# Another order for a planned attention-and-gate kernel: 117 instead of 133 changes of the array mode, the first pairs' bounds in two parts, the last output tile in two halves

## The chip, the cores and the metric

The kernel runs on one core of a Trainium2 chip. The metric is the device time of one execution in microseconds (us), as a median over executions. Of one further execution there is a profile by the hardware profiler, with the start and duration of each instruction and the landing of each transfer.

A core has five engines with a queue each: TensorE (PE in the profile; its weight loads are PEld), VectorE (DVE), ScalarE (ACT), GpSimd (POOL) and SyncE (SP), which here issues nearly all DMA transfers. An engine executes its queue in order and waits on semaphores of the others. So the order in which a program hands instructions to each engine is part of the program, and this case is about that order.

## The reference

For 4 batches, 8 heads, 768 positions and 64 features, keys are cut into 24 chunks of 32. For every query, an upper bound of its scores in each chunk is worked out from the chunk's smallest and largest key in each feature. The six chunks with the largest bounds (among the chunks that are not in the future) are kept, and softmax attention runs over them under the causal mask. The heads, side by side, are the input x of a gated unit:

```python
ub = np.sum(np.maximum(q * k_min, q * k_max), axis=-1)        # [.., 768, 24]
ub = np.where(causal, ub, -1e9)
top_chunks = np.argsort(ub, axis=-1)[..., -6:]
scores = where(chosen chunk & causal, scale * q @ k.T, -1e9)
x = softmax(scores) @ v                                       # [4, 768, 512]
gate = sigmoid(sum over 5 taps of conv_w[k] * x shifted by 4 - k)
out = (gate * (x @ w_val)) @ w_out                            # [4, 768, 512], float32
```

## The kernel before

**Tiling.** Two heads make a pair, so there are 16 pairs, and four pairs make a batch. For pair p the program creates some 60 operations, each of which is a short run of instructions on one engine. The names below are used in all that follows; the number of the pair stands behind the name, and digits behind that count parts.

- kn, qn, vn: the pair's loads (SP, lines 457 and 460). ktr, qtr: transposes of K and Q on TensorE (line 472). kev, qev: their evictions by ACT (478, 514). kred: chunk maxima and minima on DVE (484). ksm: the small arithmetic on those by GpSimd (504 to 509).
- rhi, qlo, rlo: relu(Q) and the low-order parts of Q and relu(Q), on ACT or DVE (522 to 565). Bounds must be exact enough to order chunks, so each is a sum of four products: relu(Q) high, Q high, Q low, and relu(Q) low, with chunk values. Four matmul terms form ub (590, or 605 for the pairs 0 to 3, whose form lies in `ubd`). qsb is one matmul that helps ACT to get at Q's low part in pairs 1 to 3 (530).
- top, cmp: the sixth largest bound and the comparison with it, on DVE. selT (663) transposes the comparison on TensorE, and mc copies it to SBUF, on ACT or DVE (675, 677); from pair 9 on a transposing DMA, md, does both (665).
- sc p.0 to p.5: scores of the pair in six PSUM-bank groups (692), with the selection added as a large negative number by a second matmul (697). Each is 64 rows of contraction, two heads side by side, which is a row-tiled mode of the array. ex: the exponentials by ACT (706), twelve per pair. tri: the causal diagonal by GpSimd (714). av: P times V on TensorE (735). nrm: the division, on DVE (743, 744).
- tox and xc, or from pair 8 to 14 one transposing DMA xd (765): the result transposed to xT. xw writes xT to a scratch in DRAM (778), xs reads it back in another layout into XS (782), and cv, the convolution of the gate, is 40 matmuls on tiles of 64 rows by 32 columns (793): a third mode of the array. th: the sigmoid as a tanh, on ACT (799).
- Per batch: val (816), gv (824), out (840), oe, which evicts an output tile (847, 850), and od, its store (855).

**PSUM.** There are eight banks. A score group takes two, a convolution two, and most others one, until what reads them is done.

**What sets the order.** `graph` creates the operations with their dependencies, an estimated duration and a key. The key is the number of the pair times `PERIOD`, plus an offset of the stage from `OFF`, plus one of the stage and pair from `DELTA`. `Graph.schedule` is a list scheduler: in a modelled time it starts, on each engine that is free, the ready operation with the lowest key, if a PSUM bank is free. It adds `MODE_SWITCH` where TensorE goes from one array mode to another; `mode` is "row" for sc, "col" for cv and none for all others. Then `plan` hands on the order, `fill` puts idle-time matmuls on a zero tile into TensorE's early gaps (915), and the operations are emitted in that order, so all the numbers above affect the program through the order alone, and through how many fillers fit.

The beginning also holds eight matmuls on the zero tile (line 345). In the bounds of the pairs 0 to 3, the four terms of each of five query tiles stand together:

```python
terms = [(rh, 0), (Qh, 1), (ql, 1), (rl, 0)]      # for tile i: two matmuls each
```

and the first matmul of pair 0, with the causal fill, is `identb` times `cfill`. The last output tile (batch 3, tile 5) is like every other: four matmuls of 512 columns, one eviction by DVE, one store by SP.

Of the kernel before, what the change touches and what calls it, by code (L numbers as in the profile page):

```python
# [14 lines left out]
AF = mybir.ActivationFunctionType  # L15
# [39 lines left out]
for _bi, _segs in enumerate(BANKS):  # L55
    for _col, _jt, _q0, _n in _segs:
        for _i in range(_n // 128):
# [5 lines left out]
PERIOD = 13.2487  # L63
OFF = dict(wdg=689.463, wbig=-821.57, cw=-638.386, load=-26.611, ktr=-313.189, qtr=-239.905, kev=166.913,
           qev=-383.955, ksm=148.208, spl=244.528, vc=540.922, ub=-278.308, top=-291.823, selT=-172.354,
           sc=-256.234, ex=-198.66, av=-117.315, nrm=263.685, tox=-134.594, xs=14.333, conv=-269.157,
           tanh=-393.525, val=323.303, gv=522.471, out=327.173, ev=91.258)
# [3 lines left out]

EARLY = (0, 1, 2)
# [6 lines left out]
    wdg=(-0.259, 11.176, 5.417, 0.077, -1.668, 4.13, 5.35, 1.029, 15.805, 3.045, -3.731, 0, -3.953, 0, 0, 0),  # L79
    wbig=(4.521, -1.173, -4.251, -0.71, -6.836, -7.879, -1.406, -13.108, -0.554, -12.202, 1.098, -1.574,  # L80
        -2.473, -1.919, 10.286, 15.067),
    cw=(0, 0, 1.049, 0, -3.776, -0.311, -0.92, -4.993, -0.92, -6.529, -7.915, -11.168, 0.948, 0, -8.06, 3.706),
    load=(-9.433, -20.842, -32.131, -6.001, -15.044, -1.827, -12.02, 13.514, 5.014, 13.589, 14.754, 5.081,
        -6.414, 4.609, -2.48, -7.659),
    ktr=(-2.8, -5.035, -2.262, 2.581, 0.902, 9.564, 0, 0, 10.923, 1.13, -0.491, -0.903, 0, 13.091, 0, -1.519),
    qtr=(0, -0.071, 9.102, 0, 3.757, 12.574, 5.717, -4.881, -3.114, -14.91, -6.366, 2.222, 0.471, 9.573, 4.53,
        0),
    kev=(-2.229, -2.16, 2.677, -4.88, -7.568, -10.347, 4.307, -2.668, 4.622, 3.276, -0.858, 6.192, 2.689,
        -4.962, -5.387, -2.214),
    qev=(-4.798, -6.316, 0, 0.959, 0, -3.801, -4.226, -3.069, -0.528, -1.223, 0, 0, -6.763, 0, 2.363, 0.065),  # L90
    ksm=(13.028, 3.364, 1.499, 0.759, -1.548, -11.855, -3.051, 6.295, -16.352, 0.972, -0.612, 7.732, 0, -1.146,
        0, -2.064),
# [193 lines left out]

ENG = ("PE", "ACT", "DVE", "POOL", "SP")
SEM = dict(PE=0.20, ACT=0.17, DVE=0.15, POOL=0.11, SP=0.0)
MODE_SWITCH = 0.04
DMA_HEAD, DMA_TAIL, DMA_QUEUE = 1.0, 1.3, 3.0  # L290


# [4 lines left out]
def act(n):  # L297
    return 0.051 + n / 1200.0
# [732 lines left out]
```

## Time and profile before

| | us |
|---|---|
| median of 4 runs | 189.7 |
| their range | 188.59 to 191.15 |
| the profiled execution's own time | 190.39 |
| its span, first to last instruction | 188.7 |
| TensorE busy (2994 matmuls) | 177.7 |
| ACT busy | 145.1 |
| DVE busy | 137.6 |
| GpSimd busy | 88.1 |

The granted TensorE clock was 1.000 as a mean over the span. Of the page's parts, the share of busy time tells which engine is nearest to its limit as a mean, and the row of 40 slices where along the span that holds. The chain is followed back from the last instruction and says on what the end hung. The waits say what an engine with nothing to do was waiting for. A line of the timeline has a start, a duration, engine, line, operation, output and input, the count of equal instructions that were merged, and in brackets the idle time of that engine before it. Matmuls overlap in their pipeline, so the start of one to the start of the next is what one costs, and that is shorter than the duration shown.

### The profile page before, as it was taken

What the parts mean: (1) busy time and instruction counts of PE and PEld (TensorE: products, weight loads), DVE (VectorE), ACT (ScalarE), POOL (GpSimd) and SP (SyncE); (2) the same over time, 40 slices, a digit from 0 to 9 for tenths busy, and PEclk for the clock granted to TensorE, in tenths of its full rate; (3) what the DMA queues carried; (4) which work ended last, traced back from release to release, by engine and by line L of the source; (5) the groups of instructions that cost most, each with busy time, mean ns of one, the idle gap of its engine ahead of it and who ended that gap; (6) DMA issues with size and microseconds to landing.
All of it is one profiled execution on the core that took longest, in us unless ns stands there. A gap on an engine that the chain in (4) does not pass through costs nothing.

```text
span 188.7 us, 7611 instructions
## 1 busy us (share of the span) xinstructions
PE 177.7 (94%) x2994; PEld 118.1 (63%) x2994; DVE 137.6 (73%) x452; ACT 145.1 (77%) x326; POOL 88.1 (47%) x187
## 2 busy tenths in 40 slices
PE   7889999999999999999999999999999897799992
PEld 2566768777687658667766766767665654444540
DVE  4696998799989997999996889797965322521551
ACT  4659999989979788799939998969999596156221
POOL 5336899998981851715154563538464021000000
PEclk9999999999999999999999999999999999999999
DMA  6999999999699998988998999999959979977335
GB/s 141 220 218 218 215 208 181 221 199 211 185 216 261 235 224 198 212 216 242 140 231 210 233 201 223 104 226 148 227 136 218 244 237 199 271 252 250 116 121 212
DMA packets 97105, 38.77 MB, mean 206 GB/s; under 512 B 86810, under 2 KB 91950, under 8 KB 97070
## 3 DMA queue, kind: packets, MB, share of 16 engines
q1 hardware_dynamic: 95966, 37.25, 93.9%
q0 software_dynamic: 1104, 1.05, 3.9%
q8 instruction: 23, 0.38, 0.9%
q14 instruction: 12, 0.10, 0.2%
HBM read 27.34 MB, written 9.47 MB: 195 GB/s over the span
## 4 chain that ended last, share of the span: by engine, by line
PE 75%; ACT 7%; DMA 7%; DVE 6%; issue 2%; SPq 1%; ACTq 0%; DVEq 0%
PE b L735 11%; PE b L692 11%; PE b L816 10%; PE b L472 10%; PE b L840 9%; PE b L793 8%; PE b L697 7%; PE b L590 5%; DMA XS<-scr 5%; ACT P L706 4%; DMA qn<-in_q_dram 2%; PE b L663 1%; DVE km L484 1%; PE b L760 1%; ACT Qh L514 1%
## 5 line engine op out<-in xcount | busy, mean ns | idle before, releaser
L706 ACT ACTIVATE P<-b 128x512 f16<-128x512 f32 (+2 forms) x192 | 88.9, 597 | 6.2 <-PE b L697 2.2
L714 POOL TENSOR_SCALAR_AFFINE_SELECT P<-P 128x512 f16<-128x512 f16 (+1 forms) x64 | 34.0, 552 | 43.9 <-ACT P L706 43.8
L692 PE MATMUL b<-Qh,Kh 64*128 64x128 f16 (+3 forms) x384 | 39.9, 259 | 0.6 <-ACT P L706 0.6
L697 PE MATMUL b<-MT,E 64*128 64x128 f16 (+4 forms) x352 | 37.0, 255 | 0.1
L484 DVE TENSOR_REDUCE km<-b 128x12 f32<-128x384 f32 x64 | 32.4, 547 | 6.0 <-PE b L472 3.5
L824 DVE SCALAR_TENSOR_TENSOR gv<-g,b 128x384 f16<-128x384 f32 x32 | 17.1, 548 | 15.7 <-PE b L816 14.0
L735 PE MATMUL b<-VA,P 128*128 128x65 f16 x672 | 27.7, 194 | 0.0
L735 PEld LDWEIGHTS <-P 128*128 128x128 f16 x672 | 24.4, 98 | 4.3 <-issue 2.3
L692 PEld LDWEIGHTS <-Kh 64*128 64x128 f16 x384 | 17.7, 94 | 12.8 <-issue 8.0
L799 ACT ACTIVATE g<-b 128x384 f32<-128x384 f32 x32 | 14.1, 497 | 14.1 <-PE b L793 14.0
L816 PE MATMUL b<-xT,wval 128*128 128x384 f16 x128 | 24.5, 327 | 0.0
L840 PE MATMUL b<-wout,gv 128*128 128x512 f16 x96 | 23.0, 379 | 0.0
L850 ACT ACTIVATE osb<-b 128x512 f32<-128x512 f32 x21 | 12.9, 639 | 10.6 <-PE b L840 6.7
L697 PEld LDWEIGHTS <-E 64*128 64x128 f16 x352 | 17.3, 94 | 4.6 <-issue 1.9
L793 PE MATMUL b<-XS,WD 64*32 64x384 f16 x640 | 16.5, 324 | 2.9 <-DMA XS<-scr 1.9
L478 ACT ACTIVATE Kh<-b 128x384 f16<-128x384 f32 x32 | 16.0, 532 | 3.7 <-PE b L472 2.9
L744 DVE TENSOR_TENSOR on<-b,rcp 128x384 f16<-128x384 f32 x32 | 17.8, 557 | 1.1
L514 ACT ACTIVATE Qh<-b 128x384 f16<-128x384 f32 x32 | 15.2, 508 | 3.1 <-PE b L472 3.0
L816 PEld LDWEIGHTS <-wval 128*128 128x128 f16 x128 | 11.4, 98 | 9.9 <-issue 2.6
L560 DVE SCALAR_TENSOR_TENSOR rl<-Qh,ql 128x640 f16<-128x640 f16 x16 | 14.4, 901 | 2.2 <-ACT ql L537 2.2
L472 PE MATMUL b<-ident,qn 128*128 128x128 f32 x96 | 14.7, 281 | 0.3 <-DMA qn<-in_q_dram 0.3
L472 PE MATMUL b<-ident,kn 128*128 128x128 f32 x96 | 14.3, 281 | 0.7 <-DMA kn<-in_k_dram 0.5
(87 smaller groups left out, 287.3 us busy)
## 6 DMA issues: line engine op xcount, KB each, us to landing
XS<-scr SPq DMA_DIRECT2D x32, 194.0 KB, 4.2
kn<-in_k_dram SPq DMA_DIRECT2D x32, 192.0 KB, 4.8
qn<-in_q_dram SPq DMA_DIRECT2D x32, 192.0 KB, 4.4
vn<-in_v_dram SPq DMA_DIRECT2D x16, 384.0 KB, 5.3
out_dram<-osb SPq DMA_DIRECT2D x24, 256.0 KB, 3.6
scr<-xT SPq DMA_DIRECT2D x32, 97.0 KB, 4.3
wvn<-in_moe_w_val_dram POOLq DMA_DIRECT2D x1, 512.0 KB, 8.4
wout<-in_moe_w_out_dram POOLq DMA_DIRECT2D x4, 128.0 KB, 7.5
```

What stands on the lines that cost most here:

```text
L472: t.nc.tensor.matmul(out=b[:, j * 128:(j + 1) * 128], lhsT=vv(name, p)[:, 3 * w + j, :], rhs=t.ident, is_transpose=True, start=(j == 0), s ...
L484: t.nc.vector.tensor_reduce(out=vv("km", p)[:, i, w * 12:(w + 1) * 12], in_=bank(("kn", p, w))[:, 0:HB].rearrange("p (c t) -> p c t", t=CH ...
L692: nc.tensor.matmul(out=bb[hh][:, col:col + n], lhsT=kh[HP[hh], jt * 128:(jt + 1) * 128], rhs=qh[HP[hh], q0:q0 + n], start=(si == 0), stop= ...
L697: nc.tensor.matmul(out=bb[hh][:, col + m0 - q0:col + n], lhsT=t.E[HP[hh], jt * 128:(jt + 1) * 128], rhs=mt[HP[hh], m0 - 128:q0 + n - 128], ...
L706: t.nc.scalar.activation(out=t.P[p % 2][hh][bi], in_=bank(("s", p, bi, hh))[:, 0:n], func=AF.Exp, scale=0.125 / QS)
L714: t.nc.gpsimd.affine_select(out=ap, in_=ap, pattern=[[0, n], [1, 128]], compare_op=ALU.is_ge, fill=0.0, base=0, channel_multiplier=-1)
L735: t.nc.tensor.matmul(out=b[:, qt, :], lhsT=t.P[p % 2][hh][bi][:, col:col + 128], rhs=vv("VA", p)[:, hh, jt, :], start=(jt == 0), stop=(jt ...
L744: t.nc.vector.tensor_tensor(out=vv("on", p)[:, :, hh * 64:(hh + 1) * 64], in0=b[:, :, 0:D], in1=rc.unsqueeze(2).to_broadcast([128, NT, D]) ...
L793: t.nc.tensor.matmul(out=bank(("cv", p, r))[32 * g:32 * g + 32, 0:HB], lhsT=t.WD[HP[r], g * 20 + k * 4 + p % 4, :], rhs=x[HP[r], g * XH + ...
L816: t.nc.tensor.matmul(out=k[:, 0:HB], lhsT=t.wval[:, ct, et * 128:(et + 1) * 128], rhs=t.xT[:, (4 * b_ + ct) % 8, XL + w * HB:XL + (w + 1) ...
L824: t.nc.vector.scalar_tensor_tensor(out=vv("gv", 4 * b_ + et)[:, sl], in0=vv("g", 4 * b_ + et)[:, sl], scalar=1.0, in1=bank(("val", b_, et, ...
L840: t.nc.tensor.matmul(out=k, lhsT=vv("gv", 4 * b_ + et)[:, s * 128:(s + 1) * 128], rhs=t.wout[:, et, :], start=(et == 0), stop=(et == NCT - 1))
```

## The change

1. `MODE_SWITCH` goes from 0.04 to 0.09, some estimated durations change (cwrep 0.7 to 1.5, wsplit 1.3 to 1.7, wout 2.0 to 2.2, ktr and qtr 0.33 to 0.35), and `PERIOD`, all of `OFF` and all of `DELTA` are replaced. Every engine's order is another one.
2. For pair 0, the stages from ktr to selT have fixed keys ahead of everything else (`FIRST`).
3. For the pairs 0 to 3 the bounds are emitted as ub (three terms, all five tiles) and then ur (the fourth term, relu low, all five tiles), so ub need not wait for rlo.
4. The copy mc of pair 0 is made by DVE and no longer by ACT (`MCA`).
5. The last output tile is made in two column halves: four matmuls of 256 columns each, the first evicted by DVE and stored by SP, the second evicted by ACT and stored from ACT's queue. The output tiles 2 to 5 of the last batch have keys behind everything else.
6. Seven instead of eight matmuls on the zero tile at the beginning.

```diff
-PERIOD = 13.2487
-OFF = dict(wdg=689.463, wbig=-821.57, ...
+PERIOD = 14.0000
+OFF = dict(wdg=1118.545, wbig=-917.674, ...
+FIRST = dict(ktr=0, qtr=1, kev=1, ksm=2, qev=2.5, spl=3, ub=4, top=5, selT=6)
+MCA = (1, 2)
...
-MODE_SWITCH = 0.04
+MODE_SWITCH = 0.09
...
     def key(stage, p, x=0.0):
+        if p == 0 and stage in FIRST:
+            return FIRST[stage] - 100 + x
         return p * period + off[stage] + off.get((stage, p), 0.0) + x
...
-        for _ in range(8):
+        for _ in range(7):
             t.nc.tensor.matmul(out=b, lhsT=t.warm[:, 0:128], rhs=t.warm, start=True, stop=True)
...
-        def ubd(i, p=p):
+        def ubd(i, low, p=p):
...
-                if i == 0:
+                if i == 0 and not low:
...
                 for k, (lhsT, m) in enumerate(terms):
+                    if low != (k == 3):
+                        continue
...
             for i in range(NIT):
-                G.op(f"ub{p}.{i}", "PE", 0.28 + (0.14 if i == 0 else 0), key("ub", p, 0.02 * i), ubd(i),
...
+                o = G.op(f"ub{p}.{i}", "PE", 0.21 + (0.14 if i == 0 else 0), key("ub", p, 0.02 * i), ubd(i, False),
...
+            for i in range(NIT):
+                G.op(f"ur{p}.{i}", "PE", 0.07, key("ub", p, 0.1 + 0.02 * i), ubd(i, True), r=[("rl", p), ("KB", p), ("ubh", p)], w=[("ub", p)],
                      ps=[("ub", p)])
...
-            if p in EARLY:
+            if p in MCA:
                 t.nc.scalar.copy(out=vv("MT", p), in_=h16(("sel", p))[:, 0:NIT * 128])
...
+        def lastmm(j, s=NT - 1, b_=b_):
+            def emit():
+                for et in range(NCT):
+                    t.nc.tensor.matmul(out=bank(("out", b_, s, j))[:, 0:256], lhsT=vv("gv", 4 * b_ + et)[:, s * 128:(s + 1) * 128],
+                                       rhs=t.wout[:, et, j * 256:j * 256 + 256], start=(et == 0), stop=(et == NCT - 1))
+            return emit
+
+        def lastev(j, s=NT - 1, b_=b_):
+            def emit():
+                src, dst = bank(("out", b_, s, j))[:, 0:256], vv("osb", 6 * b_ + s)[:, j * 256:j * 256 + 256]
+                if j == 0:
+                    t.nc.vector.tensor_scalar(out=dst, in0=src, scalar1=0.5, scalar2=None, op0=ALU.mult)
+                else:
+                    t.nc.scalar.activation(out=dst, in_=src, func=AF.Copy, scale=0.5)
+            return emit
+
+        def lastdma(j, s=NT - 1, b_=b_):
+            def emit():
+                (t.nc.sync if j == 0 else t.nc.scalar).dma_start(
+                    out=t.out[b_, s * 128:(s + 1) * 128, j * 256:j * 256 + 256], in_=vv("osb", 6 * b_ + s)[:, j * 256:j * 256 + 256])
+            return emit
...
         for s in range(NT):
-            x = s * 3.2
+            x = s * 3.2 + (1e5 if b_ == B - 1 and s >= 2 else 0)
+            if b_ == B - 1 and s == NT - 1:
+                for j in range(2):
...
+                continue
```

The order that results, along TensorE's queue, has 117 changes of the array mode where it had 133: the score groups stand in 46 runs and not in 54, the convolutions in 13 and not in 16. Three of the convolutions of batch 2 (pairs 8, 9, 10) stand one behind the other, and so do those of the pairs 15 and 14. On SP, the load vn0 stands ahead of qn1, and in the last third the stores od1.3 to od1.5 stand ahead of the reads xs12 and xs13. The program has 3000 matmuls where it had 2994: four more for the halves, one warm-up matmul less, three more fillers (12 and not 9).

## The prediction

> **What bounds the kernel now.** I read the page's busy shares first, then busy time by stage, then the timeline of TensorE around places where the array mode changes, and last the chain and SP's queue where the chain leaves TensorE.
>
> ```profile
> PE 177.7 (94%) x2994; PEld 118.1 (63%) x2994; DVE 137.6 (73%) x452; ACT 145.1 (77%) x326; POOL 88.1 (47%) x187
> ...
> PE   7889999999999999999999999999999897799992
> ```
>
> ```profile
> 0.00:23.00 23.00, 19.56 (x262) 13.26 (x263) 16.75 (x58) 16.59 (x38) 12.28 (x34) 1.00 1.14 201
> 23.00:53.00 30.00, 29.40 (x522) 22.27 (x521) 26.45 (x96) 29.12 (x68) 27.83 (x53) 1.00 1.05 203
> 53.00:147.00 94.00, 93.72 (x1667) 63.91 (x1666) 80.46 (x271) 81.23 (x184) 45.97 (x98) 1.00 1.05 205
> 147.00:185.00 38.00, 35.01 (x552) 18.66 (x548) 13.28 (x28) 18.21 (x39) 2.00 (x4) 1.00 0.75 212
> ```
>
> Columns of the second: stretch, length, then busy time of PE, PEld, DVE, ACT, POOL, the granted clock, the DMA share, GB/s. There are four stages. Up to 23 us loads and short chains let TensorE idle. From 23 to 53 TensorE (29.4 of 30) and ACT (29.1) are both full, so saving on one alone brings little. From 53 to 147 TensorE alone is full (93.7 of 94; ACT 81): what leaves TensorE there leaves the time. From 147 on TensorE has 3 us of holes, and ACT and DVE are half idle.
>
> **Mode changes.** What one costs is read off equal runs with different successors:
>
> ```profile
> 152.04 1.47 PE L816 MATMUL b<-xT,wval 128*128 128x384 f16 x8
> 153.44 1.01 PE L793 MATMUL b<-XS,WD 64*32 64x384 f16 x40
> 154.38 0.28 PE L692 MATMUL b<-Qh,Kh 64*128 64x256 f16 x2
> ...
> 179.99 1.46 PE L816 MATMUL b<-xT,wval 128*128 128x384 f16 x8
> 181.29 3.62 PE L840 MATMUL b<-wout,gv 128*128 128x512 f16 x16
> ```
>
> Eight val matmuls take 1.30 from their start to the next start where an output tile follows (179.99 to 181.29), and 1.40 where a convolution follows (152.04 to 153.44). So a change to another mode costs 0.10. Over all 133 changes, those without a wait cost 0.089 to 0.098, so I take 0.094. The new order has 16 fewer: 16 x 0.094 = **-1.5**. Where: up to av4.00 both orders have made 34, up to the end of pair 13's av 111 against 101, at the end 133 against 117. None of the saving falls into the first 53 us, where ACT would have eaten it; 10 fall into the stage where TensorE alone is full. The rest of TensorE's work is the same: adding the cost per operation from these rows, without warm-up, fillers and waits, gives 166.5 before and 165.0 after.
>
> **Waits of the last third.** In the third stage TensorE waits some 2 us in all, in pieces below 0.3; in the fourth the convolutions wait for their transfers:
>
> ```profile
> 163.49 1.01 PE L793 MATMUL b<-XS,WD 64*32 64x384 f16 x40 [1.02 <-DMA XS<-scr]
> ```
>
> ```profile
> 162.48 0.05 SPq L782
> 162.53 0.05 issue
> 162.58 4.28 DMA XS<-scr
> 166.87 0.14 issue
> 167.00 1.01 PE b L793 x40
> ```
>
> The convolutions of pairs 8, 11, 12 and 13 begin 0.70, 1.08, 1.09 and 0.30 late, together 3.2. The one of pair 11 is put down to ACT, and its read landed in the same 0.1 us. The chain of pair 13 took 24.3 (its av ended at 142.6, its read landed at 166.9), mostly in SP's queue:
>
> ```profile
> 147.63 1.26 SPq L765 DMA_TRANSPOSE xT<-on  x1
> ...
> 156.08 2.09 SPq L778 DMA_DIRECT2D scr<-xT  x2
> ...
> 162.07 1.10 SPq L782 DMA_DIRECT2D XS<-scr  x2
> ```
>
> In the new order I set the end of av13 to 0 and walk with these rows. cv8, cv9 and cv10 come at 0.1 to 2.7; their reads stand before xd12, whose source is done at -5.6, so they landed. SP then has md15 (comparison done at -0.5, issue 1.25), xd13 (issued at 1.1, landed 3 to 5.3 later, as the seven xd were), xs11, xw12, xw13 (at about 5 to 6, landing 4.3 later), od1.3, od1.4, and od1.5. The last waits for an eviction that ACT makes after five exponentials of pair 15: about 8.2. Only then come xs12 (8.6, landed at 12 to 13) and xs13 (9.8 to 11, landed at 13 to 15). TensorE's work until cv12 is 13.2 and until cv13 14.6. xs15 and xs14 land at 24.6 and 25.6, and cv15 and cv14 come at 26.0 and 26.9. ACT: exponentials of pair 14 end at 1.1, and those of pair 15 hold five banks at cv11, which costs 0.5. So I expect 1.0 of waits in place of 3.2: **-2.2**, with 0 (all of it returns) and -3.2 as ends.
>
> **The start.** SP now issues vn0 before qn1. 384 KB at the 201 GB/s of that stage are 1.9, so qn1 lands at 11.9 where it did at 10.1, and qtr1.0 goes from 11.14 to 12.0. Bounds: ub0 without relu low no longer stands still in the middle (0.5 at 9.8), but rlo0 and three kred still precede top0 on DVE, so cmp0 stays at 12.8 to 13.0. The copy mc0 on DVE takes 0.49 and not 0.69, and comes 0.9 earlier; ACT is 0.57 lighter, and ex0.00 goes from 16.45 to about 14.75. That gain is spent again: kev2 stands behind ten exponentials and holds two banks until 22; cmp1 stands behind cwrep (two copies of 0.81) on DVE; sc0.5 stands behind ur2, which waits for rlo2. Followed with these durations, the first scores of pair 1 end at 24.05 with 12.57 of TensorE's work done. Before, that much was done at 23.2. I take **+0.8**, with 0 and +1.9 (the whole load) as ends. Between there and 53 us ACT has 27.2 of work (512-column exponentials start 0.477 apart), so the lateness can be made up only in part; I leave it in. One warm-up matmul less and three fillers more stand in waits and cost nothing; if that cover is gone, three fillers are 3 x 0.22.
>
> The eight warm-up matmuls of 512 columns start 0.42 apart, the fillers of the same shape from 5.47 us on 0.22 apart, so TensorE's rate doubles between them. The Trainium skill, "TensorE: Matmul & The Clock Gate", Part 1, says that the clock is released after a window of about 3.4 us of sustained work. By that rule seven warm-up matmuls are at the edge; if the release slips, the first transposes run at half rate, by my estimate from that page 0.3 on the first chain. The sum stays without it, since the new order has a filler in the eighth's place.
>
> **The end.**
>
> ```profile
> 184.94 0.69 DVE L847 TENSOR_SCALAR osb<-b 128x512 f32<-128x512 f32 x1 [1.04 <-PE b L840]
> ```
>
> Behind it the store was issued at 185.66 and landed at 187.67, 2.0 later. Halves: TensorE streams as many columns, and the last eviction is by ACT with 256 columns, 0.26 to the next start and 0.42 as duration: -0.27 to -0.43. No store from ACT's queue is in this trace; the nearest rows are SP's (0.33 to issue) and GpSimd's loads (8.4 to landing, 4 times the size). I take SP's: **-0.35**, ends -0.45 and +0.5.
>
> **Sum**: -1.5 - 2.2 + 0.8 - 0.35 = -3.25. The third stage has other small waits in place of its 2 us, for which I allow -1 to +1. The profiled execution took 190.39, 1.7 beside its span, which gives 187.1; it lay 0.7 above the median of 189.7. Off the median it is 186.45: **186.5**.
>
> **Rivals.**
>
> - *Waits take the place of mode changes* (189.6). The start loses 1.9, the tail keeps its 3.2: -1.5 + 1.9 - 0.35 = 0. For it: ACT at 29.1 of 30 until 53, and scores of pairs 6 to 8 that now stand within 15.6 of TensorE's work, where ACT needs 18.2, so only free banks keep TensorE going. Against it: av of those pairs come late enough. 0.22.
> - *Slower: the reads of pairs 12 and 13 are stuck behind the stores* (192.5). The queue is in order, so xs13 waits for od1.5 and for the landing of xw13. With the largest landings seen (transpose 5.3, scratch write 7.6, read 6.9) the chain is 20.6 and cv13 waits 6.0; with the start at +1.9, the sum is -1.5 + 6.0 - 3.2 + 1.9 - 0.35 = +2.8. It is slower by 1% from a chain of about 20 on. For it: that chain took 24.3 before. Against it: SP's queue is short at that point now. 0.14.
> - *Everything fits* (184.2): no wait in the tail, start even, the other small waits less by 0.5: -1.5 - 3.2 - 0.35 - 0.5 = -5.5. 0.14.
> - *The order doesn't do what it says*: mode changes at which TensorE waits anyway cost nothing. Then half of 1.5 goes: 187.2, inside the forecast's own case.
>
> **How the numbers follow.** The forecast has 0.50, between 185.2 and 188. A measurement of this kernel tells about 1% from no change, that is 187.8 and 191.6. Faster: 0.46 of the forecast's 0.50, 0.14 and 0.05 of the first rival, 0.65. Same: 0.21. Slower: 0.14. The range, 184.2 to 190.6, leaves out most of the slower case and the lower half of the best one.
>
> **What would show it.** Right: 117 changes at 0.094, convolution waits of about 1 after pair 13's av, cv8 to cv10 without a gap, stores of the last halves from two queues, and pair 1's first scores 0.5 to 1 later. Wrong: a wait of over 2 us at cv12 or cv13 with SP idle at od1.5; ex4.51 later than 54.5 (it was 52.84); or TensorE waiting for PSUM banks at sc8.3 to sc8.5.

## The result, and the profile after

The changed kernel takes 189.99 us as a median of 44 executions (188.17 to 195.74), the kernel before, run beside it, 189.91 (63 executions, 187.98 to 192.81). The ratio is 0.9994, with a 95% interval of 0.9976 to 1.0011: no difference, where 186.5 us had been forecast. Ratios here leave out executions more than 1.5% above the fastest of their kernel, and that matters for this change: a quarter of the changed kernel's executions take more than 191.57 (before: 190.57), while the fastest quarter is below 189.05 (before: 189.26). So its lower quartile is 0.2 lower and its upper one 1.0 higher. That the spread is wider is not shown beyond chance: 12 of 44 executions are over 191 us where 8 of 63 were before, and the lowest of all belongs to the kernel before.

The profiled execution took 189.12, with a span of 187.4, so it is one of the good ones, 0.9 below the median. That of before was 0.5 above its median. The two profiles must therefore be read as two samples. First come the busy time of the engines and the first row of the slices, from the page of the changed kernel:

```profile
PE 178.7 (95%) x3000; PEld 121.0 (65%) x3000; DVE 138.6 (74%) x453; ACT 144.1 (77%) x326; POOL 86.9 (46%) x187
...
PE   7979999999999999999999999999999899999992
```

Then the busy time in the same four stretches as for the kernel before (columns: stretch, length, then PE, PEld, DVE, ACT, POOL, the granted clock, the DMA share, GB/s):

```profile
0.00:23.00 23.00, 19.93 (x238) 13.14 (x239) 14.88 (x53) 15.14 (x34) 11.59 (x33) 1.00 1.12 200
23.00:53.00 30.00, 29.20 (x527) 22.25 (x523) 27.63 (x90) 28.81 (x68) 26.89 (x49) 1.00 1.13 209
53.00:147.00 94.00, 93.53 (x1739) 65.66 (x1739) 82.17 (x284) 81.00 (x187) 46.09 (x102) 1.00 1.02 218
147.00:185.00 38.00, 36.03 (x527) 19.96 (x504) 13.96 (x28) 19.13 (x41) 2.38 (x6) 1.00 0.61 187
```

In the last stretch TensorE is busy a microsecond more than before (36.03 against 35.01). ACT in the first stretch is busy 1.45 less (15.14 against 16.59); part of that is the copy mc0, 0.69 before, which DVE makes now, and the rest comes back only in the last stretch (19.13 against 18.21).

Busy shares hide where the difference lies, so I use another measure in all that follows: TensorE's **idle time up to an operation**, which is the time at which it starts, less what all of TensorE's work before it costs (from the start-to-start times of the same operations elsewhere, with 0.094 for each change of the array mode). Cut at three operations, it gives:

| TensorE idle, us | before | after | difference | forecast |
|---|---|---|---|---|
| to the first scores of pair 1 (sc1.0) | 10.60 | 11.80 | +1.2 | +0.8 |
| from there to the end of pair 13's av | 4.39 | 5.47 | +1.1 | 0 (-1 to +1) |
| from there to the last output tiles | 3.21 | 1.31 | -1.9 | -2.2 |
| changes of the array mode (133, 117) | | | -1.5 | -1.5 |
| end of the last matmul to end of the span | 3.92 | 3.78 | -0.1 | -0.35 |
| span | 188.66 | 187.40 | -1.26 | -3.25 |

The row of the mode changes is 0.094 times their number, so it is an account and not a measurement of its own. Even between these two executions no term but that one came out as good as forecast. And the remaining 1.3 us are lost between the profiled executions and the medians (0.9 in the changed kernel, 0.5 in the one before). One place that differs from one execution to the next lies in the third row, at the three convolutions in a row, of which the forecast had said that they come without a gap. TensorE's timeline of the changed kernel:

```profile
145.49 1.87 PE L808 MATMUL b<-XS,WD 64*32 64x384 f16 x80
147.96 1.30 PE L808 MATMUL b<-XS,WD 64*32 64x384 f16 x40 [0.59 <-ACT g L814]
149.19 1.04 PE L855 MATMUL b<-wout,gv 128*128 128x512 f16 x4
```

The first 80 matmuls are cv8 and cv9. Then cv10 starts 0.75 late. The profile puts that down to ACT, but the trace shows that the last piece of the read xs10, on whose semaphore the first weight load of cv10 waits, landed at 147.82. ACT was only the last to be seen.

The end, in two halves, answers to the single DVE eviction at 184.94 of before (the last line is from the list of transfers: the count, the size, and the time from issue to landing):

```profile
182.75 1.04 PE L862 MATMUL b<-wout,gv 128*128 128x256 f16 x8
183.00 0.60 ACT L887 ACTIVATE osb<-b 128x512 f32<-128x512 f32 x1 [1.18 <-PE b L855]
183.39 0.42 DVE L870 TENSOR_SCALAR osb<-b 128x256 f32<-128x256 f32 x1 [0.61 <-PE b L862]
183.83 0.38 ACT L872 ACTIVATE osb<-b 128x256 f32<-128x256 f32 x1 [0.23 <-DVE osb L870]
184.05 0.41 SPq L877 DMA_DIRECT2D out_dram<-osb  x1
184.24 0.38 ACTq L877 DMA_DIRECT2D out_dram<-osb  x1
...
out_dram<-osb ACTq DMA_DIRECT2D x1, 128.0 KB, 2.2
```

The last eviction is 0.31 shorter (0.38 against 0.69), but the store behind it, from ACT's queue, lands 2.19 after its issue where SP's took 2.01. So 0.13 is left.

### The profile page after: what moved, and what is told of

The parts are those of the page before. It is cut to its first block, busy times and chain, and to the rows that moved or that the text cites. A ratio compares the mean times of both kernels' runs of the same rounds, so it can differ in the third digit from the quotient of the medians.

```text
span 187.4 us, 7607 instructions
## 1 busy us (share of the span) xinstructions
PE 178.7 (95%) x3000; PEld 121.0 (65%) x3000; DVE 138.6 (74%) x453; ACT 144.1 (77%) x326; POOL 86.9 (46%) x187
## 3 DMA queue, kind: packets, MB, share of 16 engines
q0 software_dynamic: 1104, 1.05, 4.3%
## 4 chain that ended last, share of the span: by engine, by line
PE 62%; DVE 16%; ACT 9%; POOL 5%; issue 3%; DMA 2%; SPq 0%; ACTq 0%; POOLq 0%; DVEq 0%
PE b L855 11%; PE b L831 9%; PE b L707 8%; PE b L750 7%; PE b L479 6%; PE b L808 6%; ACT P L721 6%; PE b L712 6%; DVE km L491 3%; PE b L597 3%; DMA XS<-scr 2%; PE b L614 2%; PE b L352 2%; DVE on L759 2%; POOL WD L448 2%
## 5 line engine op out<-in xcount | busy, mean ns | idle before, releaser
L721 ACT ACTIVATE P<-b 128x512 f16<-128x512 f32 (+1 forms) x192 | 92.0, 607 | 6.7 <-PE b L712 6.2
L729 POOL TENSOR_SCALAR_AFFINE_SELECT P<-P 128x512 f16<-128x512 f16 (+1 forms) x64 | 34.5, 562 | 36.0 <-ACT P L721 35.9
L491 DVE TENSOR_REDUCE km<-b 128x12 f32<-128x384 f32 x64 | 33.0, 547 | 10.9 <-PE b L479 5.4
L707 PEld LDWEIGHTS <-Kh 64*128 64x128 f16 x384 | 18.3, 94 | 12.0 <-issue 7.4
L831 PE MATMUL b<-xT,wval 128*128 128x384 f16 x128 | 23.6, 326 | 0.0
L855 PE MATMUL b<-wout,gv 128*128 128x512 f16 x92 | 22.0, 380 | 0.0
L485 ACT ACTIVATE Kh<-b 128x384 f16<-128x384 f32 x32 | 16.8, 582 | 4.0 <-PE b L479 3.2
L521 ACT ACTIVATE Qh<-b 128x384 f16<-128x384 f32 x32 | 15.8, 546 | 4.3 <-PE b L479 4.3
L584 POOL CAST VA<-vn 128x768 f16<-128x768 f32 x16 | 13.2, 827 | 12.3 <-PE b L750 7.0
L831 PEld LDWEIGHTS <-wval 128*128 128x128 f16 x128 | 11.7, 98 | 8.1 <-issue 1.1
L808 PE MATMUL b<-XS,WD 64*32 64x384 f16 x640 | 16.1, 324 | 0.8 <-ACT g L814 0.6
L479 PE MATMUL b<-ident,kn 128*128 128x128 f32 x96 | 15.4, 290 | 0.0
L567 DVE SCALAR_TENSOR_TENSOR rl<-Qh,ql 128x640 f16<-128x640 f16 x16 | 14.4, 897 | 0.6 <-ACT ql L544 0.5
```

The costliest lines, as they stand in the source:

```text
L479: t.nc.tensor.matmul(out=b[:, j * 128:(j + 1) * 128], lhsT=vv(name, p)[:, 3 * w + j, :], rhs=t.ident, is_transpose=True, start=(j == 0), s ...
L491: t.nc.vector.tensor_reduce(out=vv("km", p)[:, i, w * 12:(w + 1) * 12], in_=bank(("kn", p, w))[:, 0:HB].rearrange("p (c t) -> p c t", t=CH ...
L707: nc.tensor.matmul(out=bb[hh][:, col:col + n], lhsT=kh[HP[hh], jt * 128:(jt + 1) * 128], rhs=qh[HP[hh], q0:q0 + n], start=(si == 0), stop= ...
L721: t.nc.scalar.activation(out=t.P[p % 2][hh][bi], in_=bank(("s", p, bi, hh))[:, 0:n], func=AF.Exp, scale=0.125 / QS)
L729: t.nc.gpsimd.affine_select(out=ap, in_=ap, pattern=[[0, n], [1, 128]], compare_op=ALU.is_ge, fill=0.0, base=0, channel_multiplier=-1)
L808: t.nc.tensor.matmul(out=bank(("cv", p, r))[32 * g:32 * g + 32, 0:HB], lhsT=t.WD[HP[r], g * 20 + k * 4 + p % 4, :], rhs=x[HP[r], g * XH + ...
```

## The experiments

All of them change orders that were already worked out, by this helper behind the planner, so that only the named operations move (line numbers shift by a little between kernels: a convolution is L793, L808 or L809):

```diff
+def moved(order, moves):
+    """Take the operation `a` out of the order and put it directly behind (1) or ahead of (-1) `b`."""
+    for a, b, side in moves:
+        o = next(x for x in order if x.name == a)
+        order = [x for x in order if x is not o]
+        at = next(i for i, x in enumerate(order) if x.name == b)
+        order.insert(at + (side > 0), o)
+    return order
...
+    order = moved(order, MOVES)
```

### 1. Mode changes alone, both ways

In the order before, ten neighbours on TensorE are swapped, 133 to 118 changes (b_modes); in the new order eight, 117 to 132 (a_modes).

```diff
+MOVES = (('sc6.1', 'av5.11', 1), ('cv2', 'sc6.1', -1), ('val0.10', 'sc6.4', 1), ('sc7.2', 'val0.30', 1), ('cv4', 'sc8.5', 1),
+         ('cv6', 'ktr12.1', 1), ('sc10.3', 'val1.20', 1), ('val1.21', 'sc10.5', 1), ('sc6.5', 'val0.10', -1), ('sc12.4', 'av11.00', -1))
```

> The order of before, in which ten operations of TensorE between pair 4's av and pair 13's av change places with a neighbour one or two places away, so that the array mode changes 118 and not 133 times; nothing else differs. If a change of mode costs 0.094 us of a TensorE that bounds this stage, 15 x 0.094 = 1.4 us go: about 0.7% faster, and in the trace the distance from av4.00 to av13.11 shrinks by 1.4. If waits take the place of mode changes there, as the first rival of the prediction says, the time stays within 0.3 us and the waits of TensorE in that stage grow from 2 to over 3.

> The reverse on the changed kernel: its order with eight operations of TensorE between av4.00 and av13.11 put one place further, so that there are 132 mode changes and not 117. If the changes are on the path, it is 1.4 us slower than the changed kernel (about 191.3 against 190.0). If they are covered by waits, it stays at 190.0 within 0.4.

Measured: b_modes 193.48, ratio 1.0224 (1.0167 to 1.0281), so slower with 15 changes fewer. a_modes 192.46, ratio 1.0172 (1.0119 to 1.0224), which is 2.5 more than the changed kernel, for 1.4 of mode changes. The start-to-start times still give 0.088 to 0.096 for a change of mode (0.12 behind a convolution). What moves the time is waits: in the profile of b_modes, TensorE's idle time between sc1.0 and the end of pair 13's av is 10.1 in place of 4.4. One of its moves, cv2 ahead of the scores of pair 6, shows how. First ACT's, then TensorE's timeline of b_modes:

```profile
65.78 0.88 ACT L799 ACTIVATE g<-b 128x384 f32<-128x384 f32 x2 [0.19 <-PE b L793]
69.23 1.08 ACT L706 ACTIVATE P<-b 128x512 f16<-128x512 f32 x2 [2.58 <-issue]
```

```profile
66.95 1.68 PE L793 MATMUL b<-XS,WD 64*32 64x384 f16 x40
...
69.87 0.37 PE L692 MATMUL b<-Qh,Kh 64*128 64x512 f16 x1 [0.52 <-ACT P L706]
...
72.11 0.23 PE L692 MATMUL b<-Qh,Kh 64*128 64x128 f16 x2 [0.47 <-ACT P L706]
```

While TensorE makes the convolution first, ACT has no scores and stands for 2.58 us. Then ACT is late, its banks are not free, and TensorE waits for it at 69.87 and 72.11. Each move saves 0.094 or 0.19. What TensorE's scores wait for ACT in all is, before and then in b_modes (total, number of waits, longest):

```profile
PE b L692 <- ACT P L706: 0.6, 2, 0.4
PE b L692 <- ACT P L706: 3.0, 9, 0.5
```

Both kernels were made slower, the one with 15 changes fewer and the one with 15 more. So these runs show that a single move away from an order can cost more in waits than a mode change; that fewer changes as such bring waits they do not show.

### 2. The halved last tile alone

The kernel before with part 5 of the change only (the functions `lastmm`, `lastev` and `lastdma`, without the later keys of the last batch's tiles).

> The kernel before with the last output tile in two column halves alone, the second stored from ACT's queue; the order up to there is the same. The prediction's step says -0.35 us (0.2%). The profile of the changed kernel shows 3.78 from the last matmul's end to the end of the span against 3.92, so a rival says -0.14, which can't be told from nothing in the time; the trace should then show what takes back the shorter eviction.

Measured: 189.94, ratio 1.0024 (0.9986 to 1.0062): no gain can be seen, and one of 0.35 (ratio 0.9982) lies just outside the interval. Its profile shows the same as that of the changed kernel: an eviction 0.31 shorter, and a store that lands 2.18 after its issue where SP's took 2.01. The useful by-product is a second sample of the old order, which is unchanged up to the last tile: its tail waited 1.6 us and not 3.2.

### 3. SP's order of the last third alone

```diff
+MOVES = (('xs8', 'xw10', 1), ('xs9', 'xs8', 1), ('xs11', 'cv8', 1), ('xw12', 'xs11', 1),
+         ('xw13', 'xw12', 1), ('od1.2', 'xw13', 1), ('xs12', 'xd14', 1), ('xs13', 'od1.4', 1))
```

> The kernel before with SP's queue alone in another order from pair 10's scratch write on: the reads xs8 and xs9 ahead of vn15, xw13 and xs12 earlier, xs13 ahead of xw14. TensorE's order is the same. If the 3.2 us of convolution waits that the profile of before shows are there in most executions and stem from SP's order, 2 to 2.5 us go (1.2%). If they belong to that one execution, or if the transfer engines and not the order set when the reads land, less than 0.8 us go.

Measured: 191.02, ratio 1.0079 (1.0042 to 1.0115). In its profile the waits of cv8, cv11 and cv12 are gone, and 1.7 us are back at cv13 (0.44), cv14 (1.15) and cv15 (0.10). But a new hole stands far from every move, inside a convolution. TensorE's timeline of b_tail:

```profile
67.81 0.84 PE L793 MATMUL b<-XS,WD 64*32 64x384 f16 x31
70.29 0.48 PE L793 MATMUL b<-XS,WD 64*32 64x384 f16 x9 [1.63 <-issue]
```

There are 31 of 40 equal matmuls, then 1.63 us of nothing ("issue": waiting for nothing that the profile shows), then the other nine. (From the start of one matmul to the start of the next it is 1.95, and the stops below are counted so.) What came meanwhile is in the list of DMA queues, on both kernels' pages: a queue of 23 packets, 0.38 MB, of the kind "instruction". That is 16 KB a packet, for TensorE's 6,049 recorded instructions, some 256 a packet. The trace gives the time of each packet:

| profile | TensorE enters the packet before | the packet lands | TensorE stops after recorded instruction | and goes on, after the landing |
|---|---|---|---|---|
| before | 64.05 | 66.88 | 2,241 for 0.15 | 1.32 |
| b_modes | 64.09 | 66.84 | 2,241 for 0.42 | 1.46 |
| b_tail | 64.34 | 68.93 | 2,241 for 1.95 | 1.36 |
| after | 144.10 | 146.88 | 5,057 for 0.30 | 1.39 |

2,241 + 63 is 9 times 256, and 5,057 + 63 is 20 times 256; that fits if 63 instructions of the stream have no record. So this is theory F, which the expectations below use: TensorE stands when the next 256 instructions have not come. The traces allow a stricter reading. The 16 profiles of this case have 359 such boundaries. At each of them the packet landed at most 4.6 us after TensorE had entered the one before, TensorE never went on sooner than 1.32 us after the landing, and the seven smallest of these margins (1.32 to 1.47) are the seven stops that are named in this document. Where TensorE stood, it had entered the packet before 4.1 to 6.0 us earlier. The page counts these packets on the same 16 DMA engines as the data, whose share in that stage is 1.05. A convolution uses 80 instructions in 0.85 us; stretches with several of them use up 256 in 3.1 to 4.0 us, and then TensorE stands.

### 4. Moving the packets' boundary, and the first load

The first two runs cut each 512-column filler of the start into pieces, which shifts every later boundary by 144 or by 192 instructions and changes nothing else. The third puts vn0 back behind qn2, the fourth does both.

```diff
-                        t.nc.tensor.matmul(out=t.psb[k], lhsT=t.warm[:, 0:128], rhs=t.warm, start=True, stop=True)
+                        for a, b in zip(FILL_CUTS, FILL_CUTS[1:]):      # [0, 73, 146, ... 512] or [0, 57, 114, ... 512]
+                            t.nc.tensor.matmul(out=t.psb[k][:, a:b], lhsT=t.warm[:, 0:128], rhs=t.warm[:, a:b], start=True, stop=True)
...
+MOVES = (('vn0', 'qn2', 1), ('vc0', 'tri0.01', 1))
```

> The changed kernel with each of its twelve 512-column filler matmuls of the start cut into seven of 73 columns: the same columns in the same waits, but 144 more TensorE instructions ahead of everything that follows. Theory F (TensorE's instructions come in 16 KB packets, 256 instructions each, asked for when the engine enters the packet before; in the changed order three convolutions in a row, 240 instructions in 2.55 us, make the packet before the third one run out in 3.3 us, and the next one comes 3.4 to 5.9 us after it was asked for, so TensorE stands 0.75 us in the profile, at its 5,043rd recorded instruction): the boundary moves out of the three convolutions, the hole ahead of the third convolution is gone, time -0.7 (-0.3 to -1.2), 189.3 us. Rival (the hole is a wait for a tile or a bank): nothing changes, 190.0, and the hole stays ahead of the same convolution.

> The same with nine pieces of 57 columns: 192 more instructions. By theory F the next packet boundary comes to stand in the three convolutions (the packet before it would run out in 3.0 us), so a hole of 0.5 to 1.5 us is back at about 148 us, now at another matmul, with the time of the changed kernel, 190.0 (189.6 to 190.5). Rival: as the seven pieces, no difference between the two kernels, and the hole, if there is one, at the same matmul.

> The changed kernel with the load of pair 0's values (vn0) put behind the third pair's query load on SyncE, as it was before the change, and its cast (vc0) behind the first triangle mask on GpSimd. The prediction's term for the start was +0.8 and the profile shows +1.3 at the first scores of pair 1. If vn0 ahead of qn1 is the cause: pair 1's query transpose starts at about 11.1 us in place of 12.8, time -1.0 (189.0). If the start is late for another reason (the time at which the clock is released, the order of pair 1's bounds): within 0.4 of 190.0.

> Both edits together. If both theories hold and the two add up: 189.99 - 0.7 - 1.0 = 188.3 us, 0.9% under the kernel before. If neither: 190.0.

Measured: a_fill7 191.55, ratio 1.0040 (1.0007 to 1.0072); a_fill9 191.97, 1.0029 (0.9994 to 1.0065); a_vn0 190.07, 0.9990 (0.9958 to 1.0021); a_vn0_fill7 190.40, 0.9991 (0.9957 to 1.0025). None is faster than the changed kernel, so my times were wrong, and the profiles say why. TensorE's timeline of a_fill7, then of a_fill9:

```profile
146.40 1.87 PE L809 MATMUL b<-XS,WD 64*32 64x384 f16 x80
151.79 1.01 PE L809 MATMUL b<-XS,WD 64*32 64x384 f16 x40 [3.52 <-DMA XS<-scr]
```

```profile
146.95 1.87 PE L809 MATMUL b<-XS,WD 64*32 64x384 f16 x80
150.13 1.00 PE L809 MATMUL b<-XS,WD 64*32 64x384 f16 x38 [1.32 <-DMA XS<-scr]
152.37 0.50 PE L809 MATMUL b<-XS,WD 64*32 64x384 f16 x2 [1.23 <-issue]
152.80 3.12 PE L856 MATMUL b<-wout,gv 128*128 128x512 f16 x8
```

The hole ahead of cv10 did not move with the boundary, so I had put it down to the wrong cause: it is a wait for the read xs10 (theory W), 3.7 us long here, 2.9 in a_vn0 and 3.1 in a_vn0_fill7. (The profiled executions of these four kernels are all 1.2 to 3 us above their medians, so these are sizes of long executions.) Theory F holds beside it. With seven pieces nothing stops at a boundary any more; with nine the boundary falls into cv10, as expected, and TensorE stands 1.55 us two matmuls before its end, after recorded instruction 5,313, and 5,313 + 63 is 21 times 256. It goes on 1.37 after the landing. The small stop inside cv10 in the changed kernel's own profile (0.30 after instruction 5,057) stands at a boundary; the 0.75 ahead of it does not. (a_vn0 has the same 0.30 there, though 2.35 after the landing, so a stop that short may have another reason.)

In a_fill9 the eight matmuls that follow take 3.12, not 1.90: the clock is at half. The busy time by stretch of a_vn0 (columns as above) shows the same:

```profile
146.00:148.00 2.00, 1.39 (x72) 0.99 (x54) 0.51 (x1) 2.00 (x7) 0.77 (x2) 1.00 2.29 85
148.00:150.00 2.00, 0.00 (x0) 0.00 (x0) 0.00 (x0) 0.37 (x1) 0.00 (x0) 1.00 0.20 45
150.00:152.00 2.00, 1.84 (x41) 0.76 (x42) 0.00 (x0) 0.00 (x0) 0.00 (x0) 0.68 1.12 217
152.00:154.00 2.00, 2.00 (x7) 0.72 (x6) 0.00 (x0) 0.96 (x3) 0.00 (x0) 0.50 0.47 169
```

A hole of 2.9 us at 147.1 is followed by 3.4 us at half clock from 150.72 on. Here TensorE's idle time grows from 20.2 at cv10 to 22.2 at cv11, so the hole costs 4.9 and not 2.9. That accounts for some of the long executions of the changed kernel at most: of its twelve over 191 us, four have a mean clock of 0.991, which is one such stretch, and the others have 0.998 to 1.000. No profile of those was taken.

For the start, a_vn0 gives the selection transpose of pair 0 0.4 earlier (13.23 against 13.62), and the first scores of pair 1 not at all (23.93 against 23.90). The load in front was not what made the start late.

### 5. The read earlier, with and without the shift

In the changed kernel SP issues three stores of 256 KB, a value load and a scratch write between xd11 and xs10. SP's queue of the changed kernel:

```profile
135.74 1.85 SPq L780 DMA_TRANSPOSE xT<-on  x1
137.69 2.42 SPq L892 DMA_DIRECT2D out_dram<-osb  x3
140.20 0.39 SPq L464 DMA_DIRECT2D vn<-in_v_dram  x1
140.84 1.11 SPq L793 DMA_DIRECT2D scr<-xT  x2
142.00 1.11 SPq L797 DMA_DIRECT2D XS<-scr  x2
```

```diff
+MOVES = (('xs10', 'xd11', 1),)                        # a_xs10; a_xs10_vn0 has vn0 and vc0 too
+MOVES = (... as b_tail ...)  FILL_CUTS = [0, 171, 341, 512]      # b_tail_fill3
```

> The changed kernel with one operation moved on SyncE: pair 10's scratch read (xs10) stands directly behind the transpose xd11, ahead of the three stores od1.0 to od1.2, the value load vn15 and the scratch write xw11. Theory W: TensorE's hole ahead of the third convolution of the three in a row (cv10) is a wait for this read, which is issued at 142.0 to 145.9 us and lands 4.7 to 6 us later, behind three stores of 256 KB; the hole was 0.75, 1.3, 1.5, 2.9, 3.1 and 3.7 us in six profiled executions of this order, and in three of them the clock went to half for 3.4 us right behind it. Then the read now lands at 142 to 145, before 147.1 where cv10 can start, the hole is gone, and the time is -0.75 at least and about -1.5 at the median: 188.5 (187.7 to 189.2), with no execution at a mean clock of 0.991. Rival F (TensorE waits for its next packet of 256 instructions, which is late): the hole stays, 190.0.

> The same, and the load of pair 0's values behind the third pair's query load as in the run of that edit alone, where it gave 0.4 us at the first selection transpose and nothing at the first scores of pair 1. Expected as the read moved alone, within 0.4; more than 0.6 under it would say that the load does cost time at the start and that the hole had covered it.

> The kernel before with the SyncE order of the last third moved as in the earlier run of that edit (191.02), and each 512-column filler matmul of the start cut into three: 36 more TensorE instructions ahead of the rest. In the profile of the earlier run TensorE stood 1.9 us in the middle of the third convolution, at its 2,241st recorded instruction, while the 16 KB packet of its next 256 instructions landed only at 68.9 us; the same instruction stood 0.4 us in another kernel's profile. Theory F: the 36 instructions shift the packet's boundary out of the convolution into a stretch that takes 5.0 in place of 4.1 us, so this hole is gone; if it is what most executions of that order have, the time is 189.4 (188.9 to 190.0), else 190.5 to 191. Rival (that hole is contention that hits whatever is there): a hole of about the same size at about 68 us, 191.0.

Measured: a_xs10 190.42, ratio 1.0009 (0.9972 to 1.0047); a_xs10_vn0 191.36, 1.0064 (1.0027 to 1.0100); b_tail_fill3 190.26, 1.0041 (1.0001 to 1.0080). So the 188.5 expected of the read alone was missed, and two executions of a_xs10 still have a clock of 0.990 and 0.991. The read now lands some 4.5 us before cv10 needs it. TensorE's timeline of a_xs10_vn0:

```profile
146.35 2.02 PE L808 MATMUL b<-XS,WD 64*32 64x384 f16 x86
149.94 0.99 PE L808 MATMUL b<-XS,WD 64*32 64x384 f16 x34 [1.57 <-issue]
```

cv10 follows cv9 at once, and after its sixth matmul TensorE stands, in both kernels after recorded instruction 5,057 (1.20 and 1.89). The wait for the read had given the instruction packet time to come. Without it, 256 instructions are used up in 3.1 us and the packet is missing. a_xs10 also has two other long waits in its profile, for the load qn12 and for a masked tile, behind which the clock was at half once more; that profiled execution, 194.33, is no measure of the edit. b_tail_fill3 has no stop at the boundary in cv2 any more (2,241), and its ratio is 1.0041 where b_tail had 1.0079; that is the direction of theory F and not a proof in time, since the two intervals overlap. It remains above the kernel before.

### 6. Both causes at once

```diff
+MOVES = (('xs10', 'xd11', 1),)                        # and the fillers in seven pieces
+MOVES = (('xs10', 'xd11', 1), ('kn15', 'md13', 1))    # the second run
```

> The changed kernel with both edits: pair 10's scratch read directly behind xd11, and each of the twelve filler matmuls of the start cut into seven. With the read alone moved, its wait was gone from the profiles but TensorE stood 1.2 and 1.9 us inside the same convolution, both times at its 5,057th recorded instruction; with the fillers alone cut, it stood 3.7 us for the read and not at a packet's boundary. If both causes are real and stand one behind the other, only the two edits together free the place: no hole between the convolutions cv8 to cv10, and a time of 188.8 (188.2 to 189.5), about 1.2 under the changed kernel. If the place was never what decides, 190.0 or more as in the runs of each edit alone (190.42 and 191.55).

> The same, and pair 15's key load (kn15) moved on SyncE from behind the value load vn14 to directly behind md13, some 2.6 us earlier; its transpose on TensorE (ktr15) stood 0.36, 0.9 and 0.94 us in three of the profiles of this order and 0 in the others. Expected: 0 to -0.5 on the run without it. If the loads' own slack is no issue in most executions: within 0.3 of it; if the store and the transpose that are now 1.1 to 2 us later are needed: slower by up to 1.

Measured: 189.22, ratio 0.9979 (0.9939 to 1.0020), and 189.20, ratio 0.9969 (0.9938 to 0.9999). TensorE's timeline of a_xs10_fill7:

```profile
145.41 2.68 PE L809 MATMUL b<-XS,WD 64*32 64x384 f16 x120
148.03 1.90 PE L856 MATMUL b<-wout,gv 128*128 128x512 f16 x8
...
160.06 1.01 PE L809 MATMUL b<-XS,WD 64*32 64x384 f16 x40 [1.41 <-DMA XS<-scr]
```

120 matmuls in one piece: the hole is gone from the profile, here and in the two later kernels with both edits, and in none with one of them. In time, less can be told. The medians are 0.8 under the 189.99 of the changed kernel, but that was measured in another comparison. Against the kernel before, which had 189.55 in this one, the ratios give 0.2 and 0.3%, the second just outside of what can be told from nothing, and they overlap with the changed kernel's own (0.9976 to 1.0011). Nor are the long executions gone: four of twelve of a_xs10_fill7 are over 191, and one of twelve of the second. In the profiles, less is gained than what was freed, since TensorE now waits 1.4 at cv12. Its read lands at 159.9 here and at 159.8 in the changed kernel, whatever happens at cv10. A transfer reports its landing in 16 signals. In the two kernels of this section 15 of them had come by 158.1 and 158.5, and the last only at 159.9. So this wait is for one late part of a transfer, which the order on SP alone does not explain. Moving kn15 made no difference beyond 0.3.

### 7. The next read

```diff
+MOVES = (('xs10', 'xd11', 1), ('kn15', 'md13', 1), ('xw12', 'xd13', 1), ('xs12', 'xw13', 1))
```

> The run before it (pair 10's scratch read behind xd11, kn15 behind md13, fillers in seven pieces: 189.2) with one thing more on SyncE: pair 12's scratch write xw12 ahead of xs11, and its read xs12 directly behind xw13, ahead of the three stores od1.3 to od1.5. In that run the hole at the three convolutions was gone, but TensorE came to the convolution of pair 12 (cv12) 1.4 us before its read landed, at 159.9 us, as in the changed kernel, where cv12 started at 159.97 with the hole before it and hardly waited. If the chain of pair 12's transfers is what sets the time once the hole is gone: the write is issued 1.1 us earlier, the read lands at 158.6, cv12 waits 0.2, and the time is 188.1 (187.6 to 188.7), 0.9% under the kernel before. If what is freed is taken by the next read again (xs13, xs14 or xs15, or xs11, now 1.1 us later): 189.0 to 189.5.

Measured: 192.11, ratio 1.0058 (1.0020 to 1.0095). TensorE's timeline:

```profile
146.35 2.68 PE L809 MATMUL b<-XS,WD 64*32 64x384 f16 x120
...
159.51 1.01 PE L809 MATMUL b<-XS,WD 64*32 64x384 f16 x40
162.63 1.01 PE L809 MATMUL b<-XS,WD 64*32 64x384 f16 x40 [1.67 <-DMA XS<-scr]
```

cv12 does not wait any more, and cv13 waits 1.7. Its read stands behind the three stores as it did before; it landed 0.7 us later than in the second kernel of section 6, counted from the start of cv8, and TensorE is ready for cv13 1.3 sooner, since cv12 no longer holds it up. So the rival's mechanism holds here: the wait that was freed went to the next read. Its time, 189.0 to 189.5, was missed as well. The median is worse by 2.9 than that of the second kernel of section 6, of which 0.8 is in the kernel before too (190.32 in this comparison, 189.55 in that one). Why the rest is more than the 0.3 by which the waits of the tail differ in the two profiles is not settled; half of its executions had a mean clock of 0.982 to 0.991, so more of them seem to have had a stretch at half clock.

## Why the prediction was wrong, point by point

The forecast had -3.25, the two profiles give -1.26, and the medians +0.1. Two steps failed. The term for the other waits of the third stage, put at 0, came out at +1.1, the largest miss between the profiles (the start has 0.4, the tail 0.3 and the end 0.2 of it). And the tail's -2.2 rested on one execution and on a read that had not landed; that the profiles agree with it (-1.9) is luck of the two executions. The 1.35 between the profiles and the medians cannot be put down to single terms.

**Mode changes, -1.5: right in size, wrong in what it was taken for.** 16 fewer at 0.088 to 0.096 (0.12 behind a convolution) are in the trace. But they were counted as a gain of their own, with the other waits of the third stage at 0 on the mean. The old order has more changes and fewer waits: idle time between sc1.0 and the end of pair 13's av is 4.2, 4.4 and 5.1 in three profiles of the old order (6.2 in b_tail, whose stop of 1.95 lies in it), 5.5 in six of the new one and 6.0 to 9.3 in four more, where a load came late. Between the first two profiles that is +1.1 against -0.94 for the ten changes that fall there. That the waits come from the regrouping, and not from the other numbers that the change replaced, is argued and not shown; the hand-made swaps only show that a move can bring waits. This is what the first rival, "waits take the place of mode changes", had said, and its 189.6 is the nearest number; but it had put the loss into the start (1.9) and into a tail that keeps its 3.2.

**The start, +0.8: +1.2 in this pair of profiles.** Idle time at sc1.0 is 10.6 to 11.3 in five profiles of the old order and 11.7 to 12.7 in all of the new. (ex4.51 comes at 54.01; 54.5 was the mark for wrong.) The size was a third too small, and one of the reasons named was wrong: qn1 behind vn0 costs nothing there (a_vn0). ACT's timeline of the changed kernel fits the others, kev2 behind the exponentials and sc0.5 behind ur2:

```profile
21.70 0.67 ACT L721 ACTIVATE P<-b 128x384 f16<-128x384 f32 x1
22.07 1.07 ACT L485 ACTIVATE Kh<-b 128x384 f16<-128x384 f32 x2
23.51 0.69 ACT L690 COPY MT<-b 128x640 f16<-128x640 f16 x1 [0.38 <-PE b L678]
24.10 2.30 ACT L721 ACTIVATE P<-b 128x256 f16<-128x256 f32 x5
```

ACT was full there before; now it has a gap ahead of 23.51, and pair 0's last two exponentials come at 24.1 (before: 22.0). This part was only read, not tried.

**The tail, -2.2: a step that failed in its mechanism.** It had two faults. First, "cv8, cv9 and cv10 come at 0.1 to 2.7; their reads stand before xd12, whose source is done at -5.6, so they landed." That a transfer's source is done early says nothing on when the queue gets to it. SP was behind by then: its issue of xs10 ended only at -2.3 (av13's end, 145.40, is 0), and the read landed at +2.4 in the good execution, and at +3.0 to +5.3 in five others. The further walk was late as well (xs12 landed at 14.4 where 12 to 13 stood, xs13 at 15.5 where 13 to 15 stood). The forecast's "cv8 to cv10 without a gap" was met only in the kernels of sections 6 and 7. Second, the 3.2 that was to shrink came from one execution. Two other profiles whose tail keeps the old order show 1.6 and 1.8. In the new one the tail takes 1.3, 1.7, 4.0, 4.5, 5.1 and 5.1 in six profiles that leave it as it is. Most of those six are longer than their kernels' medians, so their mean isn't the tail's usual size. Whether anything is gained there at the median is therefore open; no profile settles it.

**The end, -0.35: -0.1 in the profiles, and no gain in the run of it alone.** The eviction is shorter as forecast (0.31, of 0.27 to 0.43). The part taken from SP's row was mis-sized: the store from ACT's queue lands 0.18 later after its issue. Its two ends, -0.45 and +0.5, hold both.

**What was not in the list at all.** The instruction packets: three convolutions in a row, 240 instructions in 2.6 us, need the next packet sooner than it comes. And the clock behind a long hole: the prediction weighed it at the start alone.

**The rivals.** The slower one, reads of pairs 12 and 13 stuck behind the stores, did not come at its place (cv12 waited 0.2, cv13 not at all); its mechanism came earlier, at xs10, behind od1.0 to od1.2, and in section 7 at xs13. Of the last rival, that the order doesn't do what it says, only the count is settled: there are 117 changes. Its reason, that a change where TensorE waits anyway costs nothing, was not tested, and an account that charges 0.094 to each change can't tell it from more waiting.

## What to carry to other kernels

A planner that is told a higher price for one cost can pay with another: count what the new order waits for, not only what it saves, and where two engines are nearly full, reckon that the two can cancel. A wait for a transfer, read from one execution, is one draw; look for the wait's spread over executions before its removal is priced, and walk the issuing queue from its own last known time and not from when its data are ready. When a wait is removed and the time stays, look at the same place again: two causes can stand one behind the other, and each hides the other until both are gone.

## What the runs showed of the hardware

- TensorE's instructions arrive in packets of 16 KB, 256 at a time, in a DMA queue of their own that the page counts on the same 16 DMA engines as the data. In seven profiles it stood at a boundary (0.15 to 1.95 us; the two of 0.15 and 0.30 may have another reason), always where the recorded count plus 63 is a multiple of 256, and went on 1.32 to 1.47 us after the packet's landing. At none of 359 boundaries did it go on sooner. In the seven the packet landed 2.7 to 4.6 us after TensorE had entered the one before. The Trainium skill, "Runtime: NRT & Kernel Launch", section "Terms", says that each engine has an instruction RAM that is refilled in blocks of 16 KiB; the traces agree, and add what a late block costs.
- The granted clock can fall again in the middle of a kernel. In four profiles it was 0.5 for 3.413 us while TensorE had work, beginning a whole number of times 3.413 us after it had been released (43 times in three, 30 times in one). In those four, the 3.413 us before the fall held about 0.4 to 1.1 us of matmul streaming (counted at 512 columns in 0.213 us, close to the 0.22 from one full-rate filler to the next). Windows with 1.4 to 1.6 in other profiles were followed by full clock, a hole of 3.7 us that a boundary of the windows cut in two among them. The Trainium skill, "TensorE: Matmul & The Clock Gate", Part 1, gives such a free-running window of 3413 ns and says that an idle one brings the half clock back; here a window that was about a third busy was enough. The release at the start came 4.0 to 6.8 us into the span, in profiles with seven and with eight warm-up matmuls alike, so the edge that the prediction saw in the seventh is not seen.
- A transfer's time from issue to landing is no constant: the same read, 194 KB, landed 4.0 to 6.2 us after its issue ended in six profiles of the changed order. In the five runs where it is issued ahead of the three stores it took 2.2 to 2.7. What makes it long in one of the six and short in another stays open.
